# RWKV-5 attention and a SoLU feed-forward in one kernel: ScalarE's diagonals and the first pair of half-width chunks in another order

## The chip, the cores and the metric

The kernel runs on one core of a Trainium2 chip. The metric is the device time of one execution in microseconds (us), as the median of several runs. A core has five engines, each with an instruction queue of its own that it works off in order: TensorE (PE, matrix products; its weight loads are shown apart as PEld), VectorE (DVE), ScalarE (ACT), GpSimd (POOL) and SyncE (SP), which here does nothing but issue DMA transfers. Engines wait for each other through semaphores.

## The reference

Four sequences of 768 tokens with 8 heads of 48 go through a linear attention with a decayed state, and the result through a feed-forward layer with a softmax gate and a layer norm:

```python
for t in range(S):
    cur = np.einsum('bhd,bhe->bhde', u[None] * kt, vt)
    y[:, :, t] = np.einsum('bhd,bhde->bhe', rt, state + cur)
    state = w[None, :, :, None] * state + np.einsum('bhd,bhe->bhde', kt, vt)
...
h = x @ w_in                        # x: 3072 x 384, w_in: 384 x 1024
sm = exp(h - max(h)) / sum(...)
solu = h * sm
ln = (solu - mean) / sqrt(var + 1e-6) * g_ln
out = ln @ w_out                    # w_out: 1024 x 384
```

w_in and w_out arrive as 64-bit floats; the kernel makes 32-bit weights of their words.

## The kernel before

The work is cut into N = 24 chunks of 128 tokens, numbered so that neighbours belong to different sequences (`units`). A chunk i passes through these steps, each a small function:

- `load(i, "kr")` and `load(i, "v")` (L472): DMA from HBM, issued on SP's queue, into rings of 5 (k, r) and 6 (v) buffers.
- `decay_k`, `decay_r` (POOL, L697 and L704): k and r times the powers of the decay, as `kp` and `rp`; `weigh` (POOL, L710 and L711): r*u*k; `sum_own` (DVE, L715): its sum per head, `own`.
- `diagonal(i)` (ACT, L729, eight instructions): fills the score tile `AT` with `own` on the diagonal.
- k and r are needed with the head dimension on the partitions. Chunks below FIRST = 9 are turned by PE: `turn_r` (PE L741, then DVE L742) and `turn_k` (PE L749, then a copy on ACT, L751). From chunk 9 on, `halve_rk(i)` splits the 32-bit words of `kp` (ACT, L991) and `rp` (DVE, L992) into 16-bit halves in one buffer, `turn` sends it through a transposing DMA on SP's queue (L966), and `join_rk` (DVE, L971) puts the words together again. The buffers for halves are a ring of six.
- `whole_scores` (PE, L764; chunks below WHOLE = 7) or, for pairs from chunk 7 on, `attend` = `scores` (PE, L781), `outer` (PE, L880), `take_scores` (DVE, L788, writes the scores over the masked part of `AT`) and `middle` (DVE, L898).
- `whole_y` and `whole_outer` (PE, L815, L889), or `within` and `carried` (PE, L843, L854) for pairs: the attention output. `take_y` (ACT, L864) copies it to `xT`; `update` (DVE L912 or L916 or L910, POOL L914) makes the new state.
- `ffn_in(i)` (PE, L926, twelve matmuls of some 5.3 us together) writes `h_ps`, a PSUM tile with one buffer, and ends with the exponential on ACT (L931). `unit(i)`: reciprocal and `solu` on DVE (L937, L939), then ScalarE's two passes over it, L941 and L942. `deviation` (POOL, L948, L950). `ffn_in(i+1)` can't start before `solu` of chunk i has read `h_ps`.
- `halve_ln` (ACT, L977: split of `solu`, then a turn), `join_ln` (DVE, L971), `ffn_out` (PE, L1009, eight matmuls; ACT L1011; the store on SP).
- The weights come in 14 pieces. `take_up(p)` converts a piece's low word on ACT (L522) and issues the load of a later piece; `convert_b` (DVE, L535, L537), `convert_c` (POOL, L545) and `convert_d` (DVE, L552) do the rest. `check_next` loads a piece again later for a test of its values.

Nothing schedules this automatically: the tile context is in manual mode, so the order of the calls in the source is the order in each engine's queue, and the framework adds the waits. The order is in three parts: a prologue written out call by call (L1024 to L1098), in which PE also runs idle products (`spin`); a loop over i = 2 to 6 (L1103 to L1145), where round i feeds chunk i - 2 to `ffn_in`, turns chunk i + 2 and finishes the attention of chunk i; and a loop over pairs from i = 7 on (L1174 to L1250). Its first round, i = 7, has `late` set: there the pair of chunks 7 and 8 goes through `attend` within the round, and some calls stand at other places than in later rounds. In the text below `ffn_in(5)` is the first PE work of the late round, followed by the scores of chunks 7 and 8, `ffn_out(0)`, `within` of 7 and 8, `ffn_in(6)`, `carried`, `ffn_out(1)`, the scores of 9 and 10, then in the round i = 9 `ffn_in(7)`, `within`, `ffn_out(2)`, `carried`, `ffn_in(8)`.

Of the kernel before, what the change touches and what calls it, by code (L numbers as in the profile page):

```python
# [399 lines left out]
def direct_path(  # L400
# [29 lines left out]
    nc = tc.nc  # L430
# [212 lines left out]
    def turn_table(table, out, ps):  # L643
        for a in range(HP):
            nc.tensor.transpose(ps[:, a, :], table[:, a, :], ident)
        nc.scalar.copy(out=out, in_=ps)
# [61 lines left out]
    def weigh(i, engine):  # L708
        rku = live[i]["rku"] = apool.tile([128, H, D], F32, name="rku")
        engine.tensor_mul(rku, kpads[i % NLD][:, :, 0:D], u_bc)  # L710
        engine.tensor_mul(rku, rku, rpads[i % NLD][:, :, 0:D])  # L711

    def sum_own(i):
        own = live[i]["own"] = small.tile([128, H, 1], F32, name="own")
        nc.vector.tensor_reduce(out=own[:, :, 0], in_=live[i]["rku"], axis=AX.X, op=ALU.add)  # L715

    def diagonal(i):
        X = live[i]
        if i < WHOLE:
            AT, unit_matrix = apool.tile([128, H, T], F32, name="AT", bufs=3), ident  # L720
        else:

            if (i - WHOLE) % 2 == 0:
                X["ATs"] = apool.tile([128, 2, H, U], F32, name="AT", bufs=3)
                live.setdefault(i + 1, {})["ATs"] = X["ATs"]
            AT, unit_matrix = X["ATs"][:, (i - WHOLE) % 2], same
        X["AT"] = AT
        for h in range(H):
            nc.scalar.activation(out=AT[:, h, :], in_=unit_matrix, func=ACT.Copy, scale=X["own"][:, h])  # L729
# [7 lines left out]
    def turn_r(i):  # L737
        rT = factors(i)["rT"]
        ps = psM.tile([128, HP, T], F32, tag="m", name="tr_ps")
        for a in range(HP):  # L740
            nc.tensor.transpose(ps[:, a, :], pair(rpads[i % NLD], a), ident)  # L741
        nc.vector.tensor_mul(rT, ps, fore)  # L742

    def turn_k(i):
        X = live[i]
        ps = psM.tile([128, HP, T], F32, tag="m", name="tk_ps")

        for a in range(HP):
            nc.tensor.transpose(ps[:, a, :], pair(X["kp"] if i > 0 else kpads[0], a), ident)  # L749
        if i > 0:  # L750
            nc.scalar.copy(out=X["kT"], in_=ps)  # L751
        else:
            nc.vector.tensor_mul(X["kT"], ps, back)
# [179 lines left out]
    def unit(i):  # L933
        X = live[i]
        st = small.tile([128, 8], F32, name="st", bufs=LO + 3)
        rs, tot, ss, var, rstd = (st[:, n : n + 1] for n in range(5))
        nc.vector.reciprocal(out=rs, in_=sums[:, i : i + 1])  # L937
        solu = X["solu"] = fpool.tile([128, dff], F32, name="solu", bufs=LO)
        nc.vector.scalar_tensor_tensor(out=solu, in0=X["h"], scalar=rs, in1=X["e"],  # L939
                                       op0=ALU.mult, op1=ALU.mult, accum_out=tot)  # L940
        nc.scalar.activation(out=solu, in_=solu, func=ACT.Identity, scale=-float(dff), bias=tot)  # L941
        nc.scalar.activation(out=X["e"], in_=solu, func=ACT.Square, accum_out=ss)  # L942
        X["st"] = ss, var, rstd
# [11 lines left out]
    def halves():  # L955

        return wpool.tile([128, 2 * 8 * 64, 1], U32, tag="raw", name="halves",
                          bufs=6).bitcast(U16).rearrange("p n o -> p (n o)")

    def split(words):  # L960
        return words.bitcast(U16).rearrange("p (n o) -> p o n", o=2)

    def turn(both):

        turned = halves()
        nc.sync.dma_start(out=turned.rearrange("p (n t) -> p n t", t=128), in_=both,  # L966
                          transpose=True)
        return turned.rearrange("p (o n t) -> p o n t", o=2, t=128)
# [11 lines left out]
    def join_ln(i):  # L980
        X = live[i]
        X["lnT"] = fpool.tile([128, KF, 128], F32, name="lnT")
        join(X["lnT"], X["turned"])

    def halve_rk(i):
        if i < FIRST:
            return
        X = live[i]
        both = halves()
        parts = both.rearrange("p (o e n) -> p o e n", o=2, e=2)  # L990
        nc.scalar.copy(out=parts[:, :, 1], in_=split(X["kp"].rearrange("p h d -> p (h d)")))  # L991
        nc.vector.tensor_copy(out=parts[:, :, 0], in_=split(X["rp"].rearrange("p h d -> p (h d)")))  # L992
        X["turned"] = turn(both)

    def join_rk(i):
        X = factors(i)
# [20 lines left out]
    def take_up(p):  # L1017
        nonlocal ahead
        convert_a(p)
        if ahead < len(pieces):  # L1020
            load_weights(ahead)
            ahead += 1
# [65 lines left out]
    turn_r(3)  # L1088
    take_y(2)
    turn_k(3)  # L1090
    unit(0)
    weigh(3, nc.gpsimd)
    decay_k(4)
    turn_table(fore, rdec, psM.tile([128, HP, 128], F32, tag="m", name="rd_ps"))
    update(2)
    sum_own(3)
    diagonal(3)
    weigh(4, nc.gpsimd)  # L1098


# [2 lines left out]
    for i in range(LA, LA + LO):  # L1103
        j = i - LA
        load(i + 5, "kr")
        load(i + 3, "v")
        if i > LA:
            ffn_in(j)
        before, now = now, [todo.pop(0) for _ in range(2 if todo else 0)]
        for p in before:  # L1110
            convert_c(p)
        for p in now:
            take_up(p)
        turn_r(i + 2)
        if i > LA:
            unit(j)
        sum_own(i + 2)
        turn_k(i + 2)
        decay_k(i + 3)
        if i + 3 >= FIRST:  # L1120
            decay_r(i + 3)
        weigh(i + 3, nc.gpsimd)
        if 0 <= j - 1:
            deviation(j - 1)
        if i - LO >= 0:
            halve_ln(i - LO)
        if i - LO - 1 >= 0:
            join_ln(i - LO - 1)
        if i + 3 >= FIRST:
            halve_rk(i + 3)  # L1130
        if i + 1 < WHOLE:
            whole_scores(i + 1)
            take_scores(i + 1)
        if i > LA:
            whole_y(i)
            take_y(i)
            whole_outer(i)
            update(i)
        diagonal(i + 2)
        if i == LA:  # L1140
            nc.vector.tensor_single_scalar(out=minus_g, in_=g_sb, scalar=-1.0, op=ALU.mult)
        for p in before:
            convert_d(p)
        for p in now:
            convert_b(p)  # L1145
# [28 lines left out]
    for i in range(LA + LO, N + LA + LO, 2):  # L1174
        j, l = i - LA, i - LA - LO

        late = i == LA + LO
        for n in (i + 5,) * late + (i + 6, i + 7):
            if n < N:
                load(n, "kr")  # L1180
        for n in (i + 3, i + 4):
            if n < N:
                load(n, "v")
        first, second = ([n] if n < N else [] for n in (i + 2, i + 3))
        if late:
            decay(i + 3)
            sum_own(i + 3)
            halve_rk(i + 3)
            ffn_in(j)
            unit(j)  # L1190
            attend([i, i + 1])
        decay(i + 4)
        for n in (j - 2, j - 1):
            if LO - 1 <= n < N:
                deviation(n)
        decay(i + 5)
        if l + 2 == N:
            check_sums()
        if l + 2 < N:
            halve_ln(l + 2)  # L1200
        for n in first:
            diagonal(n)
        join_ln(l + 1)
        for n in first:
            join_rk(n)
        if j < N and not late:
            ffn_in(j)
            unit(j)
            within([i, i + 1])
        if i + 4 < N and not late:  # L1210
            halve_rk(i + 4)
        check_next()
        ffn_out(l)
        if late:
            within([i, i + 1])
            ffn_in(j + 1)
        for n in (i, i + 1):
            if n < N:
                carried(n)
        if l + 3 < N:  # L1220
            halve_ln(l + 3)
        for n in (i, i + 1):
            if n < N:
                take_y(n)
        for n in (i, i + 1):
            if n < N:
                update(n)
        if late:
            unit(j + 1)
        for n in second:  # L1230
            join_rk(n)
        if j + 1 < N and not late:
            ffn_in(j + 1)
        for n in second:
            diagonal(n)
        if j + 1 < N and not late:
            unit(j + 1)
        ffn_out(l + 1)
        if late:
            halve_rk(i + 4)  # L1240
        if i + 5 < N:
            halve_rk(i + 5)
        for n in (i + 4, i + 5):
            if n < N:
                sum_own(n)
        attend([i + 2, i + 3])
        if l + 2 < N:
            join_ln(l + 2)
        if i >= N - 7:
            check_next()  # L1250
# [43 lines left out]
```

## Time and profile before

| | us |
|---|---|
| median of 14 runs | 351.43 |
| lowest and highest run | 349.21 and 356.59 |
| the profiled execution | 350.52 |
| its span, first to last instruction | 348.8 |
| PE busy in the span | 333.3 |
| ACT, DVE, POOL busy | 235.2, 208.7, 171.5 |

The granted TensorE clock was 0.997 of full speed. The profile shows one execution. Its views: busy time by engine, waits (who waited for whom: total, number, longest), the timeline (start, duration, engine, line, operation, output <- input, shapes, count, and in brackets the engine's idle time just before and what ended it), the chain of work that ended last, and windows (busy time of each engine in a stretch). "SPq" rows are DMA issues on SP's queue; their duration is the time until SP could go on. In the stretch from 130 to 312 us PE was busy without a break; DMA engines had a mean busy share of 0.36 to 1.02 there.

### The profile page before, as it was taken

To read this page: it belongs to the slowest core of one execution; us is meant where nothing else is said; L and a number is where in the kernel's file an instruction comes from. 1 tells how busy PE (TensorE), PEld (TensorE's weight loads), DVE (VectorE), ACT (ScalarE), POOL (GpSimd) and SP (SyncE) were. 2 spreads that over 40 slices of the span, in tenths; PEclk is the share of its full clock that TensorE was granted. 3 is DMA by queue.
4 is the path that set the end of the run, shared out by engine and by line. 5 is a ranking of instruction groups with operands and counts; after the bars stand their busy time and mean duration, and the time that the engine had idled before them with its cause. 6 is when DMAs were issued, how large, how long until landed. Compare 5 with 4: busy or idle time off the path is not lost.

```text
span 348.8 us, 10620 instructions
## 1 busy us (share of the span) xinstructions
PE 333.3 (96%) x4483; PEld 198.9 (57%) x4483; DVE 208.7 (60%) x379; ACT 235.2 (67%) x477; POOL 171.5 (49%) x202
## 2 busy tenths in 40 slices
PE   8989899998999799999999999999999999999993
PEld 6846556655555465565565555555555555555562
DVE  8886698877784489369378378376366062332410
ACT  4865988986774896794794794796594556456510
POOL 7788777799976098565575574540300000000000
PEclk9999999999999999999999999999999999999998
DMA  7999998379999989979979979759932533454531
GB/s 146 238 237 221 244 214 135 44 131 171 168 198 185 166 211 173 180 151 177 161 156 175 191 117 181 175 118 168 188 86 45 130 84 61 114 128 114 132 97 30
DMA packets 164742, 52.69 MB, mean 151 GB/s; under 512 B 157901, under 2 KB 161102, under 8 KB 164686
## 3 DMA queue, kind: packets, MB, share of 16 engines
q1 hardware_dynamic: 164684, 51.92, 80.0%
q8 instruction: 37, 0.61, 0.8%
q14 instruction: 19, 0.16, 0.2%
q10 hardware_dynamic: 2, 0.00, 0.0%
HBM read 26.75 MB, written 4.72 MB: 90 GB/s over the span
## 4 chain that ended last, share of the span: by engine, by line
PE 67%; DVE 8%; DMA 7%; POOL 6%; ACT 5%; SPq 3%; issue 2%; ACTq 0%; POOLq 0%; DVEq 0%
PE o_ps L1009 32%; PE h_ps L926 26%; DMA halves<-halves 4%; PE at L843 3%; PE at L854 3%; ACT AT L729 2%; PE at L781 2%; DMA raw<-in_moe_w_in_dram 2%; SPq L472 2%; DVE solu L939 2%; DVE ma L537 1%; PE kv_ps L880 1%; SPq L511 1%; POOL rku L711 1%; POOL kp L697 1%
## 5 line engine op out<-in xcount | busy, mean ns | idle before, releaser
L926 PE MATMUL h_ps<-w_in_sb,xT 128*128 128x512 f32 x288 | 130.4, 601 | 4.5 <-DVE solu L939 3.9
L1009 PE MATMUL o_ps<-w_out_sb,lnT 128*128 128x384 f32 (+1 forms) x400 | 128.3, 476 | 0.0
L1009 PEld LDWEIGHTS o_ps<-w_out_sb,lnT 128*128 128x128 f32 x400 | 74.3, 190 | 48.9 <-issue 4.3
L926 PEld LDWEIGHTS h_ps<-w_in_sb,xT 128*128 128x128 f32 x288 | 52.7, 190 | 64.8 <-issue 58.6
L931 ACT ACTIVATE e<-h_ps 128x1024 f32<-128x1024 f32 x24 | 24.6, 1024 | 40.1 <-PE h_ps L926 40.1
L977 ACT COPY halves<-solu 128x2048 uint16<-128x2048 uint16 x24 | 45.4, 1891 | 7.4 <-DMA halves<-halves 7.4
L941 ACT ACTIVATE solu<-solu,st 128x1024 f32<-128x1024 f32 x24 | 27.6, 1149 | 31.9 <-DVE solu L939 31.9
L914 POOL TENSOR_TENSOR state<-state,pw 48x192 f32<-48x192 f32 x32 | 22.8, 712 | 52.8 <-DVE state L910 51.1
L971 DVE COPY lnT<-halves 128x2048 uint16<-128x2048 uint16 x24 | 39.6, 1669 | 8.0 <-DMA halves<-halves 7.7
L948 POOL TENSOR_SCALAR st<-st 128x1 f32<-128x1 f32 x24 | 5.0, 209 | 64.2 <-ACT e L942 64.1
L710 POOL TENSOR_TENSOR rku<-kpad,u_bc 128x384 f32<-128x384 f32 x24 | 30.6, 1276 | 9.9 <-DVE own L715 9.1
L729 ACT ACTIVATE AT<-same,own 128x64 f32<-128x64 f32 x136 | 34.2, 339 | 0.0
L697 POOL TENSOR_TENSOR kp<-kpad,kdec 128x512 f32<-128x512 f32 x24 | 31.2, 1302 | 3.4 <-DMA kpad<-in_k_dram 1.5
L939 DVE SCALAR_TENSOR_TENSOR solu<-h_ps,st,e 128x1024 f32<-128x1024 f32 x24 | 30.8, 1283 | 2.1
L937 DVE RECIPROCAL st<-sums 128x1 f32<-128x1 f32 x24 | 3.8, 159 | 44.6 <-ACT e L931 44.3
L565 DVE TENSOR_REDUCE least<-mag 128x1 f32<-128x384 f32 (+1 forms) x14 | 8.5, 606 | 35.1 <-ACT mag L563 35.1
L711 POOL TENSOR_TENSOR rku<-rku,rpad 128x384 f32<-128x384 f32 x24 | 28.2, 1177 | 1.9
L1011 ACT ACTIVATE o<-o_ps,st 128x384 f32<-128x384 f32 (+1 forms) x25 | 13.9, 557 | 18.6 <-PE o_ps L1009 12.6
L971 DVE COPY rk<-halves 128x2048 uint16<-128x2048 uint16 x15 | 24.8, 1656 | 2.4 <-DMA halves<-halves 2.2
L942 ACT ACTIVATE e<-solu 128x1024 f32<-128x1024 f32 x24 | 25.4, 1057 | 0.8
L704 POOL TENSOR_TENSOR rp<-rpad,rdec 128x512 f32<-128x512 f32 x15 | 22.5, 1500 | 1.8 <-DVE halves L992 1.8
L788 DVE COPY_PREDICATED AT<-later_half,at 128x256 f32<-128x256 uint32 x34 | 12.3, 438 | 14.7 <-PE at L781 14.5
(105 smaller groups left out, 387.9 us busy)
## 6 DMA issues: line engine op xcount, KB each, us to landing
raw<-in_moe_w_in_dram SPq DMA_DIRECT2D x12, 512.0 KB, 5.8
raw<-in_moe_w_out_dram SPq DMA_DIRECT2D x16, 384.0 KB, 4.3
kpad<-in_k_dram SPq DMA_DIRECT2D x24, 192.0 KB, 4.8
rpad<-in_r_dram SPq DMA_DIRECT2D x24, 192.0 KB, 5.3
vt<-in_v_dram SPq DMA_DIRECT2D x24, 192.0 KB, 5.5
out_dram<-o SPq DMA_DIRECT2D x23, 192.0 KB, 3.1
halves<-halves SPq DMA_TRANSPOSE x39, 5.2
out_dram<-o SPq DMA_DIRECT2D x2, 96.0 KB, 2.9
```

The costliest lines, as they stand in the source:

```text
L697: nc.gpsimd.tensor_mul(X["kp"].rearrange("p h d -> p (h d)"), kpads[i % NLD].rearrange("p h d -> p (h d)"), kdec.rearrange("p a d -> p (a ...
L710: engine.tensor_mul(rku, kpads[i % NLD][:, :, 0:D], u_bc)
L711: engine.tensor_mul(rku, rku, rpads[i % NLD][:, :, 0:D])
L729: nc.scalar.activation(out=AT[:, h, :], in_=unit_matrix, func=ACT.Copy, scale=X["own"][:, h])
L926: nc.tensor.matmul(h_ps[:, ts(n, NX)], X["xT"][:, j, :], w_in_sb[:, j, ts(n, NX)], start=(j == 0), stop=(j == KD - 1))
L931: nc.scalar.activation(out=e, in_=h_ps, func=ACT.Exp, accum_out=sums[:, i : i + 1])
L939: nc.vector.scalar_tensor_tensor(out=solu, in0=X["h"], scalar=rs, in1=X["e"], op0=ALU.mult, op1=ALU.mult, accum_out=tot)
L941: nc.scalar.activation(out=solu, in_=solu, func=ACT.Identity, scale=-float(dff), bias=tot)
L942: nc.scalar.activation(out=X["e"], in_=solu, func=ACT.Square, accum_out=ss)
L971: nc.vector.tensor_copy(out=words.bitcast(U16).rearrange("p n (t o) -> p o n t", o=2), in_=turned)
L977: nc.scalar.copy(out=both.rearrange("p (o n) -> p o n", o=2), in_=split(X["solu"]))
L1009: nc.tensor.matmul(o_ps, X["lnT"][:, f, :], w_out_sb[:, f, part], start=(f == 0), stop=(f == KF - 1))
```

## The change

In the prologue and the loop over i = 2 to 6 the calls are put in another order: diagonal 3 and its row sum ahead of `unit(0)`; from round 3 on, the diagonal of chunk i + 1 stands between `turn_k(i + 2)` and `unit(j)` (before, the diagonal of i + 2 stood at the round's end); `take_up` moves to the round's end. `halve_rk` is cut in two, `halve_k` (ACT) and `halve_r` (DVE and the turn). In the late round the diagonal of chunk 8 and `halve_k(10)` come ahead of `ffn_in(5)`; `attend([7, 8])` follows `ffn_in(5)`, and only then come `halve_r(10)`, `unit(5)` and the row sum of chunk 10. The loads of v for chunks 10 and 11 move behind the turn of chunk 10; those of k and r for chunks 13 and 14, which opened the round, move behind `ffn_out(0)` and `halve_rk(11)`; `halve_rk(11)` itself moves from behind `ffn_out(1)` to behind `ffn_in(6)`. PE's queue is the same, instruction by instruction.

```diff
+    def halve_k(i):
+        X = live[i]
+        X["both"] = halves()
+        parts = X["both"].rearrange("p (o e n) -> p o e n", o=2, e=2)
+        nc.scalar.copy(out=parts[:, :, 1], in_=split(X["kp"].rearrange("p h d -> p (h d)")))
+
+    def halve_r(i):
+        X = live[i]
+        parts = X["both"].rearrange("p (o e n) -> p o e n", o=2, e=2)
+        nc.vector.tensor_copy(out=parts[:, :, 0], in_=split(X["rp"].rearrange("p h d -> p (h d)")))
+        X["turned"] = turn(X["both"])
+
     def halve_rk(i):
...
+        if FIRST <= i < N:
+            halve_k(i)
+            halve_r(i)
...
     turn_k(3)
+    weigh(3, nc.gpsimd)
+    sum_own(3)
+    turn_table(fore, rdec, psM.tile([128, HP, 128], F32, tag="m", name="rd_ps"))
+    diagonal(3)
     unit(0)
-    weigh(3, nc.gpsimd)
     decay_k(4)
-    turn_table(fore, rdec, psM.tile([128, HP, 128], F32, tag="m", name="rd_ps"))
     update(2)
-    sum_own(3)
-    diagonal(3)
     weigh(4, nc.gpsimd)
...
         for p in before:
             convert_c(p)
-        for p in now:
-            take_up(p)
         turn_r(i + 2)
+        turn_k(i + 2)
         if i > LA:
+            diagonal(i + 1)
             unit(j)
         sum_own(i + 2)
-        turn_k(i + 2)
...
             update(i)
-        diagonal(i + 2)
+        for p in now:
+            take_up(p)
...
-        for n in (i + 5,) * late + (i + 6, i + 7):
+        for n in (i + 5,) if late else (i + 6, i + 7):
             if n < N:
                 load(n, "kr")
-        for n in (i + 3, i + 4):
+        for n in (i + 3, i + 4) if not late else ():
             if n < N:
                 load(n, "v")
...
         if late:
             decay(i + 3)
+            diagonal(i + 1)
+            halve_k(i + 3)
+            ffn_in(j)
+            attend([i, i + 1])
+            halve_r(i + 3)
+            unit(j)
             sum_own(i + 3)
-            halve_rk(i + 3)
-            ffn_in(j)
-            unit(j)
-            attend([i, i + 1])
+            load(i + 3, "v")
+            load(i + 4, "v")
...
         ffn_out(l)
         if late:
+            load(i + 6, "kr")
             within([i, i + 1])
             ffn_in(j + 1)
+            halve_rk(i + 4)
+            load(i + 7, "kr")
...
         ffn_out(l + 1)
-        if late:
-            halve_rk(i + 4)
-        if i + 5 < N:
-            halve_rk(i + 5)
+        halve_rk(i + 5)
```

More of the change, by code (lines that the diff above doesn't have):

```diff
@@ L983, in join_ln @@
         join(X["lnT"], X["turned"])
-    def halve_rk(i):
[L986 to L993, printed above, removed]
+    def halve_k(i):
[8 more added lines that the diff above has]
+        X["turned"] = turn(X["both"])
+    def halve_rk(i):
+        if FIRST <= i < N:
+            halve_k(i)
+            halve_r(i)
     def join_rk(i):
@@ L1128, in direct_path @@
             join_ln(i - LO - 1)
-        if i + 3 >= FIRST:
-            halve_rk(i + 3)
+        halve_rk(i + 3)
         if i + 1 < WHOLE:
@@ L1186, in direct_path @@
             decay(i + 3)
+            diagonal(i + 1)
[4 more added lines that the diff above has]
+            unit(j)
             sum_own(i + 3)
-            halve_rk(i + 3)
-            ffn_in(j)
-            unit(j)
-            attend([i, i + 1])
+            load(i + 3, "v")
+            load(i + 4, "v")
         decay(i + 4)
```

## The prediction

> **What bounds the kernel now.** I read the engine totals first, then TensorE's (PE's) own waits, then PE's timeline up to 125 us, and last what ScalarE (ACT), VectorE (DVE) and the DMA queue did just before each gap.
>
> ```profile
> PE 333.3 (96%) x4483; PEld 198.9 (57%) x4483; DVE 208.7 (60%) x379; ACT 235.2 (67%) x477; POOL 171.5 (49%) x202
> ...
> PE h_ps L926 <- DVE solu L939: 3.9, 3, 2.0
> PE at L843 <- DVE AT L788: 1.5, 1, 1.5
> ...
> 43.91 5.39 PE L926 MATMUL h_ps<-w_in_sb,xT 128*128 128x512 f32 x12 [1.98 <-DVE solu L939]
> 70.89 5.39 PE L926 MATMUL h_ps<-w_in_sb,xT 128*128 128x512 f32 x12 [0.22 <-DVE solu L939]
> 84.97 1.80 PE L843 MATMUL at<-AT,vt 64*32 64x64 f32 x128 [1.51 <-DVE AT L788]
> 116.32 5.42 PE L926 MATMUL h_ps<-w_in_sb,xT 128*128 128x512 f32 x12 [1.74 <-DVE solu L939]
> ```
>
> PE is busy for 333.3 of 348.8 us. Of the 15.5 us left, about 7.4 lie before the first and after the last matmul, 2.6 in small waits before 28 us. The four rows above hold the rest: 1.98 + 0.22 + 1.51 + 1.74 = 5.45 us. After 116.32 the chain is PE to the end with no gap, so what an edit can gain is at most these 5.45 us, and each is worth its full length, because PE's own order is the same in both kernels.
>
> Why the first gap is there, on ACT and DVE:
>
> ```profile
> 35.06 2.45 ACT L729 ACTIVATE AT<-ident,own 128x128 f32<-128x128 f32 x8
> 37.41 1.01 ACT L522 ACTIVATE low<-raw 128x384 uint32<-128x384 uint32 x2
> 38.31 0.58 ACT L751 COPY rk<-tk_ps 128x512 f32<-128x512 f32 x1
> 38.77 2.46 ACT L729 ACTIVATE AT<-ident,own 128x128 f32<-128x128 f32 x8
> 41.12 1.02 ACT L931 ACTIVATE e<-h_ps 128x1024 f32<-128x1024 f32 x1
> ...
> 42.47 1.28 DVE L939 SCALAR_TENSOR_TENSOR solu<-h_ps,st,e 128x1024 f32<-128x1024 f32 x1
> ```
>
> ffn_in(1) ended at 33.26 + 5.42 = 38.68, but its Exp (L931) began at 41.12, behind diagonals 3 and 4. h_ps has one buffer, so ffn_in(2) waits until DVE has read it.
>
> Why the last two are there:
>
> ```profile
> 81.15 1.27 DVE L992 COPY halves<-rp 128x1024 uint16<-128x1024 uint16 x1
> 82.59 1.28 DVE L939 SCALAR_TENSOR_TENSOR solu<-h_ps,st,e 128x1024 f32<-128x1024 f32 x1
> 83.81 1.44 DVE L788 COPY_PREDICATED AT<-later_half,at 128x256 f32<-128x256 uint32 x4
> ...
> 90.19 6.32 SPq L966 DMA_TRANSPOSE halves<-halves  x2
> 102.46 7.16 SPq L966 DMA_TRANSPOSE halves<-halves  x2
> ...
> 109.85 1.90 ACT L977 COPY halves<-solu 128x2048 uint16<-128x2048 uint16 x1 [7.37 <-DMA halves<-halves]
> 111.66 2.01 ACT L729 ACTIVATE AT<-same,own 128x64 f32<-128x64 f32 x8
> 113.58 1.00 ACT L931 ACTIVATE e<-h_ps 128x1024 f32<-128x1024 f32 x1
> ```
>
> The scores of chunks 7 and 8 are taken (L788) behind own(10), split and unit, at 83.81, though PE had them by 77.2. And the split of chunk 4's rows waits 7.37 us for a turn, with the diagonal and Exp of chunk 7 behind it.
>
> **The change, part by part.** Steps are start to start, from ACT's and DVE's rows: Exp 1.00 (its read 0.10 more), Identity 1.18, Square 1.05, kT copy 0.47, xT copy 0.37, diagonal 2.35 (1.92 half width), two conversions 0.91, split of solu 1.80, split of kp 0.95; DVE: reciprocal 0.20, solu 1.28, row sum 0.46, two predicated copies 1.26. No instruction is added or taken away; all of it is order.
>
> *First gap.* ACT now does diagonal 3 after the rdec copy, at 31.6, then unit 0's two passes (33.96 to 36.19), kT copy (36.66) and conversions (37.57), so chunk 1's Exp starts when ffn_in(1) is done, 38.7 instead of 41.12. DVE follows with reciprocal and solu to 41.3. PE without its gap reaches ffn_in(2) at 43.91 - 1.98 = 41.93, so all 1.98 goes, with 0.6 to spare. DVE puts row sum 3 ahead of solu(0), which ends at 32.78; ffn_in(1) needs it at 33.26, so PE hides this 0.46. With that cover gone it would cost 0.46.
>
> *Chunks 2 to 5.* Each PE round is some 9.25 (53.13 to 62.38). Behind Exp ACT has 1.10 + 0.47 + 2.35 + 1.18 + 1.05 + 0.37 + 0.91 = 7.43, done before the next Exp; the diagonal covers DVE's reciprocal and solu (1.5). DVE's predicated copies now wait for the diagonal's end, about 1 us after solu, and are needed a round later. ACT's conversions (take_up) move to the end of the round, where DVE's own half of them (L535, L537) already stood, so POOL's additions wait for DVE as before; DVE's last two w_out rows end near 75.0, against ffn_out(0) at 75.9. In the round before ffn_in(5) the split of chunk 0 comes on top: 7.43 + 1.80 = 9.23 of 9.25. So I take 0.1 of the 0.22 as gained; PE reaches ffn_in(5) at 70.89 - 1.98 - 0.1 = 68.8. Bounds: 0 to 0.22.
>
> *Third gap.* From there ACT runs without a break: Exp 4 at 66.0, kT, half diagonal 7, unit 4, split 1, kp split 9, xT, half diagonal 8, kp split 10, Exp 5 at 77.7. The kp splits need POOL's kp(9) (about 68.7) and kp(10) (about 76.5, behind the state products as at 76.11 now). DVE takes the scores when diagonal 8 is done (76.6): copies end at 77.5, mids (1.45) at 79.0, rp split 10 at 79.6, then solu(5) at 81.2. PE needs the copies at 81.3 (within) and solu(5) at 83.0 (ffn_in(6)). So the 1.51 goes, and solu(5), now behind four copies and four mids, still has 1.8 to spare: this spare is the price of putting scores first.
>
> *The queue.* SP's order changes most: the turn of rk(10) goes ahead of the loads kr(13), kr(14), v(10) and v(11). It starts at about 80 and not at 90.19; a turn lands 5.2 to 8.2 us after its issue, so rk(10) is there by 88 instead of 96.4 (PE wants it at 96). SP now waits for this turn's inputs (DVE's rp split, 79.6), and v(10), v(11), then turn 2, the check load, out(0), kr(13), turn rk(11), kr(14), turn 3, out(1) and turn rk(12) stand behind it. v(10) issues at some 83 and lands 5.2 later (median of v loads then); PE's kv needs it at 96.5. kr(13) lands near 95 and kr(14) near 101, where POOL's rp(13) still waited for DVE at 96.64 to 98.48, and where their splits stand at 110 and 118. Hidden, with 10 us of cover; a load later than that would hold POOL.
>
> *Fourth gap.* kp split 11 now stands ahead of split 3 and turn 3 goes out near 96 (ACT 92.3; turn of rk(11) at 91, about 3.5 us of issue each). It took 8.2 us when it followed the check load and out(0) (97.72 to 105.9), 5.3 to 6.2 elsewhere: it lands at 101.3 to 104.2, and I take 102.5. Split 4 waits for it, then 1.80 + 1.92 to Exp 7, so Exp 7 at 106.3 (bounds 105.1 to 108.0), solu(7) ends at 109.0 (107.7 to 110.7). ffn_in(8) is due at 116.32 - 1.74 - 1.51 - 1.98 - 0.1 = 111.0. The 1.74 goes, with 0.3 to 3.3 to spare.
>
> The page "DMA: Bandwidth & Descriptors" of the Trainium skill, in "Latency and other measured facts", gives a DMA transpose 261 GB/s; as an estimate the 512 KB of a turn would then take 2.0 us, turn 3 would land before 99, and the sum would be no different, since the gap is closed anyway. No row here shows a turn landing in under 4.3 us.
>
> One row speaks against packing POOL and DVE closer: POOL's second product of L711 took 1.94 at 71.81, under DVE's lnT copy, and 1.01 elsewhere. One such meeting more moves kp(10) by 0.9, and Exp 5 with it, inside the 1.8. The skill's page "SBUF — State Buffer" ("SBUF: two separate sides") goes further: of the two, the loser is blocked for the other's whole instruction. By that it would be the copy's 1.8, an estimate, just at the limit, and the sum the same or 0.1 worse.
>
> *Sum.* 350.52 is the profiled execution's time (span 348.8, 1.7 around it). 350.52 - 1.98 - 0.10 - 1.51 - 1.74 = 345.2. The median of the runs stands 0.91 above that execution, so 346.1. I add 0.1 for edges: 346.2.
>
> **Rivals.** (A) *One late gap stays*: turn 3 at its slow end plus an SP or ACT slip of over 0.3, or the check load ahead of it; 1.0 to 2.0 us come back, 347.2 to 348.2. For: the one turn of 8.2 us and DMA engines at a share of 1.11 from 100.7 to 116.3. Against: rk(10)'s early turn takes one of the three out of that stretch. (B) *ACT becomes the bound* from 66 to 78, where it has no idle: Exp 5 or kp(10) over 2 us late gives a gap at ffn_in(6) in place of the one at within; 348.2 to 349.6. (C) *Nothing to measure*: the gaps reappear behind other names, since PE is one in-order queue: 349.7 to 353.2, middle 351.4. Against: three gaps have separate owners. (D) *Slower*: with PE 5 us earlier, the DMA side no longer keeps up in the paired stage, and the wait of 109.85 (a split waiting for a turn) recurs in each of its seven pairs at 1.74 apiece: 346.2 + 7 x 1.74 = 358.4; it decides from the fifth recurrence (354.9). For: DMA shares of 0.91 to 1.02 from 130 to 208. Against: there SP waits for ACT's o (51.2 us), not for the engines.
>
> **How the numbers follow.** Forecast 0.55, A 0.18, B 0.09, C 0.11, D 0.07. The predicted time is the forecast's, 346.2; its own range is 344.8 to 347.2 (0.9 for the runs' scatter below). The range 344.8 to 349.6 takes in A and B, 0.82. What differs by under 0.5%, 349.7 to 353.2, can't be told from no change. So faster 0.55 + 0.18 + 0.09 = 0.82, same 0.11, slower 0.07.
>
> **What would show it.** Right: PE's waits for solu and AT after 30 us sum to under 0.5; Exp of chunk 1 within 0.2 of ffn_in(1)'s end; copies of chunks 7 and 8 done before within is due; turn of rk(10) issued within 1 us of DVE's split; PE's first ffn_in after ffn_out(2) follows carried with no gap. Wrong: a gap over 0.5 at ffn_in(5), (6) or (8), a new PE wait on a load or a turn, or gaps in the paired stage.

## The result and the profile after

| | before | after |
|---|---|---|
| median, runs taken together with the changed kernel | 351.8 us (47 runs) | 346.7 us (10 runs) |
| a second set of runs | 351.41 us (17 runs) | 346.68 us (6 runs) |
| span of the profiled execution | 348.8 us | 346.4 us, again 344.2 us |

The ratio is 0.9872, with a 95% interval of 0.984 to 0.9904; in the second set 0.9879 (0.9825 to 0.9932). The forecast was 346.2. The time is right to 0.5 us, but the profile shows that it isn't made up as forecast. First the totals and TensorE's waits (total, number, longest) of the profile that came with the result:

```profile
PE 333.4 (96%) x4483; PEld 198.5 (57%) x4483; DVE 209.5 (60%) x379; ACT 234.5 (68%) x477; POOL 173.8 (50%) x202
...
PE h_ps L926 <- POOL w_in_sb L545: 2.1, 3, 1.3
PE tk_ps L749 <- POOL kp L697: 1.8, 2, 1.5
PE h_ps L926 <- DVE solu L939: 1.6, 1, 1.6
```

The wait for AT is gone, and of the three for solu one is left. The 2.1 us on w_in_sb are new, but they lie ahead of 30 us, where no queue had changed. TensorE's timeline of the same profile:

```profile
35.72 5.42 PE L926 MATMUL h_ps<-w_in_sb,xT 128*128 128x512 f32 x12
44.31 5.42 PE L926 MATMUL h_ps<-w_in_sb,xT 128*128 128x512 f32 x12
71.11 5.39 PE L926 MATMUL h_ps<-w_in_sb,xT 128*128 128x512 f32 x12
83.59 1.48 PE L843 MATMUL at<-AT,vt 64*32 64x64 f32 x128
85.00 5.42 PE L926 MATMUL h_ps<-w_in_sb,xT 128*128 128x512 f32 x12
114.24 5.42 PE L926 MATMUL h_ps<-w_in_sb,xT 128*128 128x512 f32 x12 [1.55 <-DVE solu L939]
```

These are ffn_in(1), (2) and (5), `within`, ffn_in(6) and (8). Rows without brackets have no gap before them: the first three gaps of before are gone, the fourth shrank from 1.74 to 1.55. ffn_in(1) came 2.46 us later than before's (33.26). The opening was late in this execution; a second profile of the same kernel has it at 32.69.

So stages are compared by distances between ffn_in's starts, which leave the opening's own length out:

| profile | ffn_in(1) starts | (1) to (5) | (5) to (8) | (8) to the end |
|---|---|---|---|---|
| before | 33.26 | 37.63 | 45.43 | 232.5 |
| after | 35.72 | 35.39 | 43.13 | 232.2 |
| after, second profile | 32.69 | 36.15 | 43.38 | 232.0 |

The second profile gained 1.48 + 2.05 = 3.53 us in the two stages that the change touches. That is less than the 4.7 to 5.1 us between the medians. The rest is in the granted clock, which every run lists. The 53 runs of the kernel before that were made beside the experiments fall into three groups: 22 with a mean clock of 0.995 to 0.999 (median 350.05), 20 with 0.992 to 0.994 (351.89) and 11 with 0.988 or 0.989 (354.44). Of the changed kernel's 16 runs 13 have 0.995 or more, with a median of 346.62. At the same clock the change is worth 350.05 - 346.62 = 3.43 us, which agrees with the 3.53 of the stages; the other 1.3 to 1.7 us come from runs that no longer lose clock. Where that clock goes is shown with the second experiment.

What holds ffn_in(8) now, from SP's queue, ScalarE and VectorE of the first profile after:

```profile
94.60 4.94 SPq L966 DMA_TRANSPOSE halves<-halves  x1
99.64 0.82 SPq L472 DMA_DIRECT2D kpad<-in_k_dram  x1
100.55 0.53 SPq L472 DMA_DIRECT2D rpad<-in_r_dram  x1
101.18 4.33 SPq L966 DMA_TRANSPOSE halves<-halves  x1
...
107.77 1.90 ACT L977 COPY halves<-solu 128x2048 uint16<-128x2048 uint16 x1 [6.98 <-DMA halves<-halves]
109.58 2.02 ACT L729 ACTIVATE AT<-same,own 128x64 f32<-128x64 f32 x8
111.50 1.00 ACT L931 ACTIVATE e<-h_ps 128x1024 f32<-128x1024 f32 x1
...
112.89 1.28 DVE L939 SCALAR_TENSOR_TENSOR solu<-h_ps,st,e 128x1024 f32<-128x1024 f32 x1
```

The turn of rk(11) held the queue for 4.94 us, the loads of chunk 14 for another 1.5, and only then came turn 3 (101.18), whose split had been ready since 94.27. Split 4 writes one of the six buffers for halves, and its wait ended when turn 3 landed (107.77); diagonal(11), Exp 7 and solu(7) stood behind split 4.

### The profile page after: what moved, and what is told of

Read it like the earlier page. It is cut to its first block, busy times and chain, and to the rows that moved or that the text cites. A ratio compares the mean times of both kernels' runs of the same rounds, so it can differ in the third digit from the quotient of the medians.

```text
span 346.4 us, 10629 instructions
## 1 busy us (share of the span) xinstructions
PE 333.4 (96%) x4483; PEld 198.5 (57%) x4483; DVE 209.5 (60%) x379; ACT 234.5 (68%) x477; POOL 173.8 (50%) x202
## 4 chain that ended last, share of the span: by engine, by line
PE 74%; POOL 9%; DMA 5%; SPq 4%; ACT 4%; issue 2%; DVE 1%; POOLq 0%; ACTq 0%; DVEq 0%
PE o_ps L1016 32%; PE h_ps L926 30%; PE at L854 3%; DMA raw<-in_moe_w_in_dram 3%; PE at L843 3%; SPq L472 3%; PE at L781 2%; DMA halves<-halves 2%; POOL kp L697 2%; SPq L511 2%; POOL rp L704 2%; POOL rku L710 2%; POOL rku L711 2%; ACT AT L729 2%; PE kv_ps L880 1%
## 5 line engine op out<-in xcount | busy, mean ns | idle before, releaser
L971 DVE COPY lnT<-halves 128x2048 uint16<-128x2048 uint16 x24 | 38.4, 1614 | 10.5 <-DMA halves<-halves 10.2
L711 POOL TENSOR_TENSOR rku<-rku,rpad 128x384 f32<-128x384 f32 x24 | 31.1, 1297 | 1.9
L704 POOL TENSOR_TENSOR rp<-rpad,rdec 128x512 f32<-128x512 f32 x15 | 21.2, 1412 | 0.0
```

What stands on the lines that cost most here:

```text
L704: nc.gpsimd.tensor_mul(X["rp"].rearrange("p h d -> p (h d)"), rpads[i % NLD].rearrange("p h d -> p (h d)"), rdec.rearrange("p a d -> p (a ...
L971: nc.vector.tensor_copy(out=words.bitcast(U16).rearrange("p n (t o) -> p o n t", o=2), in_=turned)
```

## The experiments

Each batch had its own runs of the kernel before; ratios are to those. "Gap" is TensorE's idle time ahead of the named work in the kernel's profile.

**The two halves of the change.** The first kernel has the changed early part and the late round of before, with diagonal(8) at the head of that round (its old place is gone); the second has the old early part and the changed late round.

```diff
...
         if late:
             decay(i + 3)
             diagonal(i + 1)
-            halve_k(i + 3)
+            sum_own(i + 3)
+            halve_rk(i + 3)
             ffn_in(j)
-            attend([i, i + 1])
-            halve_r(i + 3)
             unit(j)
-            sum_own(i + 3)
-            load(i + 3, "v")
-            load(i + 4, "v")
+            attend([i, i + 1])
...
```

> Only the prologue and the loop over i = 2 to 6 are as in the changed kernel; the late round is as before (diagonal 8 opens it, since the loop no longer makes it). Theory (each gap has its own owner): the gaps at ffn_in(2) and ffn_in(5) are gone (2.2 us), but the late conversions on ACT hold POOL's kp(9) back, so that row sum 10 (DVE, behind POOL's products of chunk 10, at about 83 us) holds split, unit and the copies of the scores: the gap at within grows from 1.5 to 2.5 to 3.5 us, the one at ffn_in(8) stays at 1.5 to 2. Time 0.3 to 1.5 us under before, ratio 0.996 to 0.999. Rival (the parts simply add): gap at within 1.5 as before, 2.2 us gained, ratio 0.993 to 0.994.

Measured: 349.73 us, ratio 0.9971 (0.9938 to 1.0004). The gap at ffn_in(2) is 0.58 instead of 1.98, the one at ffn_in(5) is gone, but the one ahead of `within` is 3.22 instead of 1.51. The early part's gain runs into the next wait; alone it is worth almost nothing. At ffn_in(8), where 1.5 to 2 was expected, no gap is left: TensorE ran more slowly behind the 3.22 (more on this below), and from ffn_in(5) to (8) this profile takes 46.81 us, where before takes 45.43.

```diff
...
-        turn_k(i + 2)
         if i > LA:
-            diagonal(i + 1)
             unit(j)
         sum_own(i + 2)
+        turn_k(i + 2)
...
-        for p in now:
-            take_up(p)
+        diagonal(i + 2)
```

> Only the late round is as in the changed kernel; prologue and loop are as before. Theory: gaps 2.0 at ffn_in(2) and 0.2 at ffn_in(5) stay, the one at within is gone (also the half microsecond that within's own matmuls lost), the one at ffn_in(8) stays at 1 to 2 us, since turn 3 still stands behind the turn of chunk 11 and the loads of chunk 14. 1.5 to 2.5 us under before, ratio 0.993 to 0.996. Rival (the late round only works with the early one shifted): a gap of over 0.5 us at within or ffn_in(6), ratio 0.996 to 1.000.

Measured: 349.31 us, ratio 0.9927 (0.988 to 0.9974). The gaps at ffn_in(2) and (5) are 1.98 and 0.21, as in before, the one ahead of `within` is gone, and the one at ffn_in(8) is 2.42, above the 1 to 2 expected. Windows of its profile (stretch in us, length, busy time of each engine, granted clock, DMA share, GB/s) show what a gap can cost beyond its length:

```profile
41.09:43.07 1.98, 0.00 (x1) 0.03 (x1) 1.61 (x4) 1.29 (x5) 1.98 (x3) 1.00 0.82 214
43.07:50.15 7.08, 7.08 (x14) 3.03 (x15) 5.26 (x11) 5.38 (x13) 5.06 (x7) 0.76 1.16 234
...
113.30:115.75 2.45, 0.04 (x4) 0.00 (x0) 1.62 (x5) 0.82 (x3) 0.93 (x1) 1.00 1.09 179
115.75:122.90 7.15, 7.15 (x13) 3.18 (x14) 3.65 (x7) 7.00 (x12) 2.05 (x3) 0.76 1.40 160
```

Behind each of the two gaps the clock is 0.76, and the twelve matmuls of ffn_in take 7.08 and 7.11 us instead of 5.42: 1.66 and 1.69 us more. The first kernel's profile has the same behind its 3.22 (0.79 to 0.85 for 8.7 us). The profile of before has gaps of the same length and the full clock behind them, so it happens in some executions only. How often goes with the longest gap:

| kernel | longest gap after 30 us | runs with a mean clock under 0.9945 |
|---|---|---|
| early part alone; late part alone; unit ahead of attend | 3.22; 2.42; 3.50 | 7 of 10; 5 of 10; 9 of 12 |
| before | 1.98 (three over 1.5) | 31 of 53 |
| after; split of k later; product of r(4) later | 1.55 and 1.80; 2.13; 1.70 | 3 of 16; 2 of 6; 1 of 6 |
| the six others below | 0.30 to 1.12 | 0 of 40 |

No run tried the gap's length alone, so this table is a connection over kernels that differ in other ways too. The gaps are those of one or two profiles of each kernel, the clocks those of all runs. The Trainium skill's page "TensorE: Matmul & The Clock Gate" ("HAM oscillation — how this bites in real kernels") warns of gaps of over some 3.4 us in TensorE's work, after which its clock is halved. Half speed for 3.4 us would cost 1.7, an estimate from the page, which fits the measured 1.66 and 1.69. As the length of gap to fear, 3.4 us doesn't fit: 1.98 was enough here, and 3.50 in another profile left the clock at 1.00.

The traces show where it happens. In each of the 14 the granted clock changes only at whole multiples of 3.41 us after it first became full, and the low stretches on the way, three in all, are each 3.41 us at 0.50. Windows on these borders, four of the late part's profile and one of the kernel with the 3.50:

```profile
40.75:44.16 3.41, 1.43 (x35) 0.85 (x24) 2.91 (x7) 2.69 (x6) 3.33 (x4) 1.00 0.88 199
44.16:47.57 3.41, 3.41 (x6) 1.34 (x5) 3.29 (x9) 3.41 (x10) 2.03 (x4) 0.50 1.25 193
...
112.42:115.83 3.41, 0.99 (x69) 0.83 (x57) 2.58 (x5) 1.78 (x6) 1.81 (x1) 1.00 1.04 176
115.83:119.24 3.41, 3.41 (x4) 1.39 (x5) 0.47 (x1) 3.38 (x5) 0.00 (x0) 0.50 1.44 178
...
109.62:113.03 3.41, 1.44 (x96) 1.28 (x96) 2.06 (x2) 3.30 (x11) 2.73 (x2) 1.00 0.97 204
```

TensorE idles for 1.98 and 2.42 us in the first and third of them, and for 2.10 in the window that precedes the first kernel's low stretch. No window of the 14 profiles with 1.97 us of idle time or less is followed by a low one. The borders cut before's gap of 1.98 into 0.81 and 1.17 and the 3.50 into 1.97 and 1.53, so what these traces show is idle time within one window, and a gap of the same length costs or not by where it falls. Three cases don't fix the limit to 0.01 us.

**Was the opening late because of the change?** The changed kernel once more, without an edit.

> The changed kernel once more, unaltered. Up to the 27th microsecond its engines' orders are those of the kernel before, and in the profile on record ffn_in(1) began at 35.72 us, where three kernels with the same opening (the experiments that keep the early part) began it at 32.40 to 32.78 and the kernel before at 33.26. Theory (the 2.5 us belong to one execution: a late weight at the opening): this profile begins ffn_in(1) at 32.3 to 33.5, its span is 343 to 345, the gap ahead of ffn_in(2) is 0.4 to 0.7 as in those kernels, the gap at ffn_in(8) is 1.2 to 2.0; the ratio to before is 0.985 to 0.990. Rival (the change itself makes the opening late): ffn_in(1) begins after 35 again.

Measured: 346.68 us, ratio 0.9879 (0.9825 to 0.9932). ffn_in(1) starts at 32.69, so the 2.46 us belonged to one execution. In this profile the gap at ffn_in(2) is 0.71 and the one at ffn_in(8) is 1.80. Its span of 344.2 and its gaps are within or 0.01 off what was expected. Ten profiles here are of kernels with the changed early part as it is; two of them have a late opening (35.72, and 34.48 with the loads at their old places), and eight have a gap of 0.42 to 0.75 at ffn_in(2). The first profile after is one of the two without it.

**What is left of the first gap.** VectorE and POOL in the second profile of the changed kernel, ahead of solu(1), and then the kernel before at the same place:

```profile
35.93 0.36 DVE L535 TENSOR_SCALAR ma<-raw 128x384 uint32<-128x384 uint32 x1
36.32 1.25 DVE L537 SCALAR_TENSOR_TENSOR ma<-raw,ma 128x384 uint32<-128x384 uint32 x1
37.49 1.15 DVE L535 TENSOR_SCALAR ma<-raw 128x384 uint32<-128x384 uint32 x1
38.68 1.25 DVE L537 SCALAR_TENSOR_TENSOR ma<-raw,ma 128x384 uint32<-128x384 uint32 x1
39.85 0.68 DVE L742 TENSOR_TENSOR rk<-tr_ps,tab 128x512 f32<-128x512 f32 x1
40.45 0.15 DVE L937 RECIPROCAL st<-sums 128x1 f32<-128x1 f32 x1
...
35.94 1.21 POOL L710 TENSOR_TENSOR rku<-kpad,u_bc 128x384 f32<-128x384 f32 x1
37.23 1.20 POOL L711 TENSOR_TENSOR rku<-rku,rpad 128x384 f32<-128x384 f32 x1
38.39 1.12 POOL L545 TENSOR_TENSOR ma<-ma,low 128x384 uint32<-128x384 uint32 x1
```

```profile
38.95 0.56 DVE L537 SCALAR_TENSOR_TENSOR ma<-raw,ma 128x384 uint32<-128x384 uint32 x1
39.43 0.35 DVE L535 TENSOR_SCALAR ma<-raw 128x384 uint32<-128x384 uint32 x1
39.82 1.26 DVE L537 SCALAR_TENSOR_TENSOR ma<-raw,ma 128x384 uint32<-128x384 uint32 x1
...
37.47 1.02 POOL L711 TENSOR_TENSOR rku<-rku,rpad 128x384 f32<-128x384 f32 x1
39.66 1.00 POOL L545 TENSOR_TENSOR ma<-ma,low 128x384 uint32<-128x384 uint32 x1 [1.17 <-DVE ma L537]
```

The same conversion takes 0.35 or 0.56 where POOL is idle, 1.15 or 1.25 where POOL is in an instruction: it then ends 0.21 (L535) or 0.42 us (L537) behind POOL's end, each time. In the changed kernel VectorE begins these conversions earlier (3.24 us behind ffn_in(1)'s start instead of 5.30), which puts three of them, and not one, beside POOL's work. The four together take 4.0 us here, 2.5 in before, and 3.2 and 3.6 in the two profiles without a gap, where two of the four stand beside POOL. This is the lock of the page "SBUF — State Buffer" ("SBUF: two separate sides"), by which the one that comes second waits for the other's whole instruction; the rows agree with it. The test takes the last thing ahead of the reciprocal away:

```diff
...
-        turn_r(i + 2)
+        product = turn_r(i + 2, hold=i == LA + 1)
         turn_k(i + 2)
         if i > LA:
             diagonal(i + 1)
             unit(j)
+        if product:
+            product()
```

> The changed kernel with one VectorE instruction moved: the product of the turned r(4) with its table (0.68 us, it stood straight ahead of the reciprocal) goes behind solu(1). Theory (the rest of the first gap, 0.71 us in the second profile of the changed kernel, is VectorE's own queue: two weight pieces' conversions of 0.36, 1.25, 1.15 and 1.25 us and this product, after which the reciprocal came 1.2 us behind Exp 1's end): the gap ahead of ffn_in(2) falls to 0 to 0.2; ratio 0.985 to 0.987. Rival (Exp 1 on ScalarE still releases it): the gap stays at 0.4 to 0.7, ratio as the changed kernel's, 0.987 to 0.990.

Measured: 345.35 us, ratio 0.9841 (0.9795 to 0.9888). No gap at ffn_in(2); ffn_in(1) to (5) takes 35.47 instead of 36.15. Exp 1 was in time; VectorE's own queue held solu(1). The medians alone can't tell this kernel from the changed one, the profile's gap can.

**The third gap: which edit did it?** First `unit(5)` back ahead of the scores.

```diff
             ffn_in(j)
+            unit(j)
             attend([i, i + 1])
             halve_r(i + 3)
-            unit(j)
```

> The changed kernel with unit(5) ahead of the scores' copies of the first pair and of the split of r(10) again; nothing else. Theory (the third gap went because the copies of scores 7 and 8 on VectorE no longer stand behind solu(5)): the copies end 1.0 to 1.4 us behind the start at which within is due, the gap ahead of within is 0.8 to 1.6, the first gap and the one at ffn_in(8) stay as in the changed kernel; ratio 0.990 to 0.993. Rival (the earlier Exp 5 from diagonal(8)'s move suffices): gap under 0.4, ratio 0.986 to 0.989.

Measured: 350.3 us, ratio 0.9985 (0.995 to 1.0021): nearly the whole gain of the change is lost, more than expected, and at another place. Ahead of `within` only 0.42 comes back, while the gap at ffn_in(8) grows to 3.50. SP's queue of this kernel, with ffn_in(5) at 68.76:

```profile
80.01 0.51 SPq L472 DMA_DIRECT2D rpad<-in_r_dram  x1
84.22 2.02 SPq L966 DMA_TRANSPOSE halves<-halves  x1
...
101.59 4.42 SPq L966 DMA_TRANSPOSE halves<-halves  x1
```

The split of r(10) now stands behind solu(5), copies and mids on VectorE, so the queue stood still from 80.5 to 84.22 for the turn of rk(10); in the changed kernel's second profile (ffn_in(5) at 68.84) it went out at 80.73. Turn 3 goes out at 101.59 instead of 99.18 and lands at 108.10 instead of 105.75. From ffn_in(5) to (8) this kernel takes 2.42 us more, and 9 of its 12 runs have the low clock on top. The order of `attend` matters less for the scores than for the split behind it.

So `unit(5)` alone owns only 0.42 of the 1.51 ahead of `within`, less than the theory's 0.8 to 1.6. The rival's earlier Exp 5 isn't the reason either: it starts 9.1 us after ffn_in(5)'s start here and 8.6 in before. VectorE in before shows what else stood ahead of the copies:

```profile
80.68 0.55 DVE L715 TENSOR_REDUCE own<-rku 128x8 f32<-128x384 f32 x1 [3.97 <-POOL rku L711]
```

The row sum of chunk 10 waited 3.97 us for POOL, with the split of r(10), `unit(5)` and the copies behind it. This kernel leaves row sum and split behind the copies, so by elimination the other 1.09 us are theirs; the early part alone has both ahead again, its row sum waits 5.63 us, and its gap is 3.22.

Then the cut of `halve_rk` in two, undone:

```diff
-            halve_k(i + 3)
             ffn_in(j)
             attend([i, i + 1])
+            halve_k(i + 3)
             halve_r(i + 3)
```

> The changed kernel with the two halves of the split of chunk 10 together again behind the first pair's copies: on ScalarE the copy of k (1.05 us) then comes behind Exp 5 instead of ahead of it; nothing else moves. Theory (the cut of the split in two buys nothing by itself, since Exp 5 has 0.8 us to spare before VectorE gets to solu(5) and the copy of r on VectorE ends after either): the turn of rk(10) is issued within 0.4 us of where the changed kernel has it, 11.9 us after ffn_in(5)'s start, the gap at ffn_in(8) is 1.4 to 2.0, ratio 0.986 to 0.990. Rival (it opens the queue): the turn goes out over 1 us later and the gap at ffn_in(8) is over 2.5.

Measured: 347.11 us, ratio 0.9878 (0.9826 to 0.9931). The turn of rk(10) went out 11.87 us after ffn_in(5)'s start (80.25 against 68.38); the gap at ffn_in(8) was 2.13, a little above the 1.4 to 2.0 expected. The cut by itself buys nothing that these runs can tell.

And the loads back at the head of the late round:

```diff
-        for n in (i + 5,) if late else (i + 6, i + 7):
+        for n in (i + 5,) * late + (i + 6, i + 7):
...
-        for n in (i + 3, i + 4) if not late else ():
+        for n in (i + 3, i + 4):
...
-            load(i + 3, "v")
-            load(i + 4, "v")
...
-            load(i + 6, "kr")
...
-            load(i + 7, "kr")
```

> The changed kernel with the loads kr(13), kr(14), v(10) and v(11) back at the head of the late round, the rest kept. Theory (the loads' move is a small part: it lets the turn of rk(10) out earlier, and what it saves in front of turn 3 is taken back by kr(14)): the turn of rk(10) is issued 5 to 8 us later than in the changed kernel, against the start of ffn_in(5); the gap ahead of within stays gone; the gap at ffn_in(8) is 1.4 to 2.6; ratio 0.987 to 0.991. Rival (the loads' move brought the third gap's gain, since the turns came out of the queue): a gap of over 1 us ahead of within or ffn_in(6), ratio over 0.992.

Measured: 347.98 us, ratio 0.989 (0.9838 to 0.9942), 1.3 above the changed kernel in the same batch. TensorE's gaps and ScalarE's wait:

```profile
97.78 1.32 PE L781 MATMUL at<-rk 48*64 48x64 f32 x61 [1.07 <-ACT xT L864]
114.64 5.42 PE L926 MATMUL h_ps<-w_in_sb,xT 128*128 128x512 f32 x12 [1.12 <-DVE solu L939]
...
95.17 1.90 ACT L977 COPY halves<-solu 128x2048 uint16<-128x2048 uint16 x1 [3.15 <-DMA halves<-halves]
```

The third gap stays gone, so the loads' move didn't bring it. The turn of rk(10) was issued 19.6 us after ffn_in(5)'s start instead of 11.9, split 3 had to wait for it to land, and the xT copies behind split 3 came late for the scores of 9 and 10 at 97.78. The gaps sum to 2.19 in two places where 1.4 to 2.6 in one was expected; from ffn_in(5) to (8) that is 44.08 us, 0.70 above the changed kernel's second profile. From ffn_in(8) to the end this profile takes 233.2 us instead of 232.0, 0.45 of it a gap at 330.87; whether that belongs to the edit isn't known.

**The fourth gap: queue, or ring of buffers?** The load of chunk 14 behind turn 3:

```diff
             halve_rk(i + 4)
-            load(i + 7, "kr")
...
             halve_ln(l + 3)
+        if late:
+            load(i + 7, "kr")
```

> The changed kernel with the load of k and r of chunk 14 moved behind turn 3. Theory (SP's in-order queue owns the fourth gap): turn 3 issues 1.5 us earlier, the split that waits for it and Exp 7 too, and the gap at ffn_in(8) falls from 1.55 to 0 to 0.4 us; ratio to before 0.983 to 0.986. Rival (the DMA engines are full, and a turn lands when they get to it): turn 3 lands within 0.5 us of where it did, gap over 1.1 us, ratio as the changed kernel's, 0.987.

Measured: 344.39 us, ratio 0.9825 (0.975 to 0.99, four runs). The gap at ffn_in(8) is 0.30; turn 3 landed 35.51 us after ffn_in(5)'s start instead of 36.66 to 36.91.

Turn 3 ahead of the turn of rk(11):

```diff
             ffn_in(j + 1)
+            halve_ln(l + 3)
             halve_rk(i + 4)
...
-        if l + 3 < N:
+        if l + 3 < N and not late:
             halve_ln(l + 3)
```

> The changed kernel with split and turn 3 ahead of split and turn of chunk 11's rows. Theory (queue order): turn 3 issues at about 95 instead of 101 us, lands at 101 to 103, the split behind it no longer sets Exp 7, which follows ffn_in(7) or the new turn's place in DVE's queue; the gap at ffn_in(8) is gone (under 0.2 us); the turn of chunk 11 then lands at 106 to 108 and its join on DVE stands ahead of solu(7), which is the closest to holding PE. Ratio to before 0.982 to 0.985. Rival (DMA engines full): as long as two turns and the loads have to land first, the gap keeps over 1 us.

Measured: 347.29 us, ratio 0.9893 (0.9859 to 0.9927): slower than the 0.982 to 0.985 expected. TensorE and VectorE of its profile:

```profile
102.48 1.92 PE L843 MATMUL at<-AT,vt 64*32 64x64 f32 x128 [0.78 <-DVE AT L788]
105.50 5.43 PE L1016 MATMUL o_ps<-w_out_sb,lnT 128*128 128x384 f32 x16 [1.11 <-DVE lnT L971]
...
99.80 0.69 DVE L994 COPY halves<-rp 128x1024 uint16<-128x1024 uint16 x1 [7.31 <-DMA halves<-halves]
```

The gap at ffn_in(8) did go, but now the split of rk(12) waits for turn 3 to land, and VectorE stood 7.31 us in it, with the scores of 9 and 10 and the joining of chunk 2's rows behind. The wait changed engines.

Split 4 behind Exp 7, with the queue as it was:

```diff
-        if l + 2 < N:
+        if l + 2 < N and l != 2:
             halve_ln(l + 2)
...
             ffn_in(j)
+            if l == 2:
+                halve_ln(l + 2)
             unit(j)
```

> The changed kernel with split 4 on ScalarE moved behind diagonal(11) and Exp 7; nothing else. In the changed kernel split 4 waited for turn 3 to land (6.98 us, 107.77) because the six buffers of halves were taken, and diagonal(11) 2.02, Exp 7 1.00 and solu(7) stood behind it. Theory (what holds ffn_in(8) is that wait on ScalarE, not the landing itself): Exp 7 ends within 1.3 us of ffn_in(7)'s end, solu(7) starts straight behind the two copies of the turned halves on VectorE, 111.5 on the old clock, and the gap of 1.55 falls to 0 to 0.4; ratio 0.982 to 0.986. Rival (turn 3 on VectorE holds it as well, or the later split puts the wait at ffn_out(4)): a gap of over 1 us stays there or in the next 20 us, ratio 0.986 to 0.990.

Measured: 344.86 us, ratio 0.9827 (0.977 to 0.9884). ScalarE and VectorE of its profile:

```profile
102.03 1.02 ACT L931 ACTIVATE e<-h_ps 128x1024 f32<-128x1024 f32 x1 [1.82 <-PE h_ps L926]
105.36 1.90 ACT L977 COPY halves<-solu 128x2048 uint16<-128x2048 uint16 x1 [2.21 <-DMA halves<-halves]
...
105.36 1.65 DVE L971 COPY lnT<-halves 128x2048 uint16<-128x2048 uint16 x1 [4.41 <-DMA halves<-halves]
106.89 2.12 DVE L971 COPY rk<-halves 128x2048 uint16<-128x2048 uint16 x1
109.15 1.28 DVE L939 SCALAR_TENSOR_TENSOR solu<-h_ps,st,e 128x1024 f32<-128x1024 f32 x1
```

Turn 3 lands as late as before (105.36, 36.77 us after ffn_in(5)'s start), but Exp 7 runs straight behind ffn_in(7), and the gap is 0.32. What held ffn_in(8) was split 4's wait for a buffer in front of Exp 7. What is left is VectorE's two copies behind the landing.

**Together.**

> The changed kernel with both edits that each took the gap at ffn_in(8) to 0.30 to 0.32: the load of chunk 14 behind turn 3, and split 4 behind Exp 7. Theory (turn 3 lands 1.2 us earlier and nothing on ScalarE waits for it ahead of Exp 7, so solu(7) ends over 0.8 us before it is due): gap 0 at ffn_in(8), and none new up to ffn_in(10); ratio 0.980 to 0.983. Rival (something else, the copies of the turned halves on VectorE or a later turn, holds it): a gap of 0.3 or more there or behind, ratio no better than 0.983.

Measured: 344.5 us, ratio 0.9799 (0.9756 to 0.9843). No gap at ffn_in(8), solu(7) ends 1.2 us ahead of it; ffn_in(5) to (8) takes 41.51 instead of 43.38.

> The kernel of load 14 and split 4 moved, with the product of r(4) behind solu(1) as well. Theory (all four gaps and what was left of them are then gone, and TensorE has no wait over 0.2 us between its 30th and 300th microsecond): span 341 to 342 if the opening is on time, ratio 0.978 to 0.981, 0.5 to 0.7 us below the kernel without the product's move. Rival (the ceiling is elsewhere): a new wait, ratio no better than 0.981.

Measured: 343.78 us, ratio 0.9778 (0.9736 to 0.982), the best of all and 0.7 below the one without the product's move. The span of 342.4 is above what was expected by 0.4, and one gap of 0.50 stayed at ffn_in(2), where none over 0.2 was expected: VectorE's four conversions took 1.44, 1.25, 1.16 and 1.24 in this execution, all four beside POOL. So moving the product shortens VectorE's queue by 0.68 and doesn't always suffice; moving conversions away from POOL's products wasn't tried.

## Why the prediction was right, and where not

The second profile after starts ffn_in(5) at 68.84, the prediction had 68.8, so its times can be laid beside the forecast's. By its own signs it holds in part: Exp 1 came within 0.2 of ffn_in(1)'s end and the copies were done in time, but TensorE's waits for solu and AT after 30 us sum to 2.51 (1.55 in the first profile), not to under 0.5, and the gap at ffn_in(8) is one of those listed under "Wrong".

- *TensorE's order is the same, and a gap closed is worth its length.* Right, and too low: the ceiling of 5.45 left out some 0.6 us in the stage from ffn_in(5) to (8), 43.38 - 1.80 = 41.58 without gaps, against 45.43 - 1.51 - 1.74 = 42.18 in before. `within` is 0.32 of it (1.80 in before, 1.48 after); the rest isn't located. It also left out the clock that a gap can cost.
- *First gap, "all 1.98 goes, with 0.6 to spare".* The step on ScalarE was right: Exp 1 starts 0.1 us behind ffn_in(1)'s end. "DVE follows with reciprocal and solu" failed: VectorE's four conversions and a product stood ahead of the reciprocal, and the step didn't price them. 1.27 us came instead of 1.98, and all of it only in the two profiles where two of the four conversions, not three, ran beside POOL.
- *0.1 of 0.22 at ffn_in(5).* All 0.22 went.
- *Third gap.* Right step by step: copies end at 77.4 (forecast 77.5), Exp 5 starts at 77.94 (77.7), solu(5) ends at 81.1 (81.2), `within` starts at 81.33 (81.3), with no gap at `within` or ffn_in(6).
- *The queue.* The turn of rk(10) went out at 80.73, not at "about 80"; the turns then held SP for 3.8 to 4.6 us and not "about 3.5 us of issue each". The turn of rk(11) went out at 92.76 instead of 91 and held SP for 4.61 instead of 3.5; with the loads of chunk 14 turn 3 went out at 99.18, not at "near 96".
- *Fourth gap, "the 1.74 goes, with 0.3 to 3.3 to spare".* Wrong, for that one term. From issue to landing 6.6 us (6.5 assumed; no turn in the traces landed in under 4.2, so the estimate of 2.0 doesn't hold here), from landing to Exp 7 3.73 (3.8): all the rest held. Landing at 105.75 instead of 102.5 and ffn_in(8) due 0.6 earlier than the 111.0 forecast turn a spare of 2.0 into a gap of 1.80. This is rival A's mechanism, one late gap; the upper bounds given for Exp 7 (108.0) didn't reach the measured 109.48, since they varied the landing and kept the issue time.
- *The median "0.91 above that execution".* Carried over as a constant, which it isn't. Of before's 53 later runs 31 lost clock, and at full clock their median, 350.05, is 0.47 below that execution; after the change 3 of 16 lost it. An offset remains: the changed kernel's full-clock median of 346.62 is 0.73 above its second profiled execution (345.89).

The sum by what was measured, from before's 350.05 at full clock: 350.05 - 1.27 - 0.22 - 1.51 - 0.6 + 0.06 = 346.5, against 346.62. The forecast's 346.2 was near it because two terms that fell short (the fourth gap by 1.8, the first by 0.7) met three that it had wrong the other way: 0.6 in the stage, 0.9 of offset, and 0.5 by which the profiled execution lay above the median at full clock. That the total came out within 0.5 us is luck of signs; that most of it comes from the first and third gaps is not. Rivals B and D didn't come about: ScalarE put no gap at ffn_in(6), and from ffn_in(8) to the end TensorE waits for no turn, in 232 us as in before. C, the gap that comes back under another name, is what the early part does alone (3.22 ahead of `within`).

## What to carry to other kernels

An in-order DMA queue has to be summed issue by issue, with the durations of the stretch that the work is moved into. When the buffers of a ring are taken, put what needs none ahead of what waits for one: that was worth as much here as shortening the queue (a gap of 0.32 against 0.30). Price everything that stands ahead of the releasing instruction on its own engine, and ask what an instruction will run beside once it starts earlier. A gap in TensorE's timeline cost 1.66 and 1.69 us beyond its length in one profile and nothing in others, so compare runs by their granted clock before explaining a median.

## What was not expected of the hardware

A transposing DMA held its issuing queue for 1.7 to 5.7 us and landed 4.2 to 8.3 us after its issue, with the same shape each time. Idle time of 1.98, 2.10 and 2.42 us within one window of 3.41 us was followed by 3.41 us at half the clock, and 1.97 was not. An integer conversion of 0.35 us on VectorE took 1.15 to 1.44 beside POOL. The opening started ffn_in(1) anywhere from 32.17 to 35.72 us with the same orders up to the 27th microsecond; in the latest TensorE had waited 2.1 us for weights from POOL.
